# Decode attention with a gated unit: gate's last product in one column tile, the queries' matrix in one load, the output matrix in six

## The chip, the cores and the metric

One core of one Trainium2 chip. Times are microseconds (us) of device time; the profiled execution counts from the start of its span. PE is TensorE, DVE VectorE, ACT ScalarE, POOL GpSimd, SP SyncE, whose queue issues almost all DMA.

## The reference

```python
xn = _layernorm(x)                                   # x: 512
q = (xn @ wq)                                        # 512 -> 32 heads of 128
scores = einsum("bhqd,bhkd->bhqk", q, k_cache) * 128 ** -0.5     # 8192 keys a head
s = softmax(scores) @ v_cache, heads side by side, @ wo          # 4096 -> 512
g = silu((sigmoid(xn @ w_gate) * (xn @ w_up)) @ w_down)          # 512 -> 1376 -> 512
return x + s * g
```

All is float32. One token is decoded, so nearly all time goes into reading the keys, the values and the weights once.

## The kernel before

Three slots in SBUF hold 8 MB each. Heads go in 16 pairs; a pair's keys and a pair's values fill one slot each. Keys alternate between slots 0 and 1, values use slot 2. Before the first keys, slot 2 holds `wq` and then `w_down`, slot 0 holds `w_gate` and `w_up`; at the end `wo` goes into the slot of the pair before the last.

SP issues the loads in program order, each behind a wait that its slot is free: `wq` (two loads, L194 and L197, each with two of the four rows that a partition holds), `w_gate`, `w_up`, keys 0, `w_down` (L322, once all queries are spread), keys 1 (L345, once the product with `w_up` is done), values 0 (L372, once `gated`, the last product of gate, is done), then keys i behind `summed[i - 2]` and values i - 1 behind `valued`. A load waits behind every load ahead of it in this queue.

VectorE first normalizes x (L261 to L280; x itself comes through ACT's queue, L241). It then scales the four rows of `wq` in each partition by x and adds them up in place (`in_place`, L295 to L298, the fourth in eight column pieces at L308), PE sums over partitions and spreads, ACT copies to `q_all`. The same way go `w_gate` and `w_up` (L336 to L344). Then VectorE turns the hidden row into `hid` (L357, L362) and goes on to the scores of pair 0 (L416, L417).

Gate's last product (L365) is 13 matmuls of a 128 x 1 column of `hid` against 128 x 512 of `w_down`, each in one of four column tiles of PE, so that four run side by side and leave four partial rows. ACT copies them (L370), `column_sums` adds them on PE and spreads a quarter of the row on each of four partition groups of `big[1]`, ACT takes the sigmoid (L374), and VectorE multiplies after pair 1 (L462).

At the end `wo` comes as 32 rows of 128 x 512; row r is multiplied by column r of `o_all`. `W_ENDS` says where its loads end. Rows below `W_FOLD` go either to VectorE (`W_DVE`, two chains that are added at L526) or as 1 x 512 products to PE (`W_PE`, with the column tile). `to_fold` (L497) adds both into `s_tmp`; `fold` sums its partitions on PE into `acc`. Rows from `W_FOLD` on go straight into `acc`, a row in four products of 128 columns; the fold stands after the row before the last. VectorE then multiplies by gate and adds x (L548, L550).

PE's notes are recorded by `Later` and played at the end, so all its rows stand at L38.

Of the kernel before, what the change touches and what calls it, by code (L numbers as in the profile page):

```python
# [9 lines left out]
AF = mybir.ActivationFunctionType  # L10
# [3 lines left out]
P = 128  # L14
# [37 lines left out]
def kernel(  # L52
# [14 lines left out]
    D = x.shape[-1]  # L67
    F = w_gate.shape[1]
    KT = D // P
# [3 lines left out]
    NG = 4  # L73
    GP = P // NG
    GC = D // NG
    QT = 512
# [5 lines left out]
    SLOT = NB * Dh  # L82
    HALF = (slice(0, HP), slice(HP, P))

    FP = F // P
    FL = F - FP * P
    FW = FP * GP
    FC = FL // GP
    assert F <= 3 * QT and FL % GP == 0 and 2 * KT * F <= SLOT and (FP + FC) * D <= SLOT // 2

    W_ENDS, W_FOLD = (12, 20, 24, 28, 30, 31, 32), 28
    W_PE = [*zip(range(5), [0] * 5), *zip(range(12, 15), [1] * 3), *zip(range(20, 22), [2] * 2), *zip(range(24, W_FOLD), (0, 1, 2, 3))]
    W_DVE = [r for r in range(W_FOLD) if r not in [r for r, _ in W_PE]]
    V_CUT, K_CUTS = NB // 2, {NP - 2: (NB * 3 // 4,), NP - 1: (NB * 23 // 32,)}

    N_SEMS = 36
    DVE, ACT, SP, POOL = nc.vector, nc.scalar, nc.sync, nc.gpsimd
    PE = Later(nc.tensor)
    pe_only = OrderedEngineSet([nc.tensor.engine])
# [2 lines left out]

    sems = [nc.alloc_semaphore(f"s_{i}") for i in range(N_SEMS)]
    s_out = nc.alloc_semaphore("s_out")

    def sb(name, *shape):
        return nc.alloc_sbuf_tensor(name, [P, *shape], F32)[:]
# [11 lines left out]
    x_row, g_row = sb("x_row", GC), sb("g_row", GC)  # L119
    ones, ident = sb("ones", P), sb("ident", P)  # L120
# [12 lines left out]
    hid = o1[:, :(FP + FC) * GP].rearrange("p (c i) -> p c i", i=GP)  # L133
# [6 lines left out]
    big, po, wide = banks[:2], banks[2], banks[3:]  # L140
# [6 lines left out]
    def semaphore(name):  # L147
        return unused.pop(0)
# [11 lines left out]
    pe, dve, act, pool = (Steps(n) for n in ("s_pe", "s_dve", "s_act", "s_pool"))  # L160
    loads = {}

    def load(eng, name, dst, src, *after):
        wait(eng, *after)
        if name not in loads:
            loads[name] = [semaphore(f"s_{name}"), 0]
        loads[name][1] += 16
        ins = eng.dma_start(dst, src)  # L168
        if not tc.compiled:
            tc.no_tile_sem_insts.add(ins.ins.name)  # L170
        ins.then_inc(loads[name][0], 16)
        return loads[name][0], loads[name][1]

    def wait(eng, *steps):
        for s in steps:
            if s is not None:
                eng.wait_ge(*s)
# [9 lines left out]

    xv = x.rearrange("a b d -> (a b d)")
    wq_t = slots[2].rearrange("p (k c) -> p k c", k=KT)
    wq_v = wq.rearrange("(p k) c -> p k c", k=KT)  # L190
    def load_queries(n):
        return load(SP, f"wq{n}", wq_t[:, n:n + 2, :], wq_v[:, n:n + 2, :])

    ld_wq = [load_queries(0)]  # L194
    tc.close()
    tc.compile()
    ld_wq.append(load_queries(2))  # L197
    wg_t, wu_t = (slots[0][:, n * KT * F:(n + 1) * KT * F].rearrange("p (k f) -> p k f", f=F) for n in range(2))
    ld_g = load(SP, "wg", wg_t, w_gate.rearrange("(p k) f -> p k f", k=KT))
    ld_u = load(SP, "wu", wu_t, w_up.rearrange("(p k) f -> p k f", k=KT))  # L200
# [1 line left out]
    def rows_of(src, i):  # L202
        rows = src.rearrange("b h s d -> (b h s) d")[2 * i * S:2 * (i + 1) * S, :]
        return rows.rearrange("(p j) d -> p (j d)", p=P)
# [8 lines left out]
    def cols(j):  # L213
        return slice(j.start * Dh, j.stop * Dh)
# [7 lines left out]
    def load_values(i, cut, *after):  # L222

        wait(SP, *after)
        for j in cut:
            sem = s_val[j.start // V_CUT]
            SP.dma_start(slots[2][:, cols(j)], rows_of(v_cache, i)[:, cols(j)]).then_inc(sem, 16)  # L227
# [34 lines left out]
    t = dve(DVE.reduce_sum(st[:, 0:1], x_col, axis=AX.X))  # L262
    wait(PE, t)
    t = pe(PE.matmul(pt[:, 0:1], ones, st[:, 0:1], start=True, stop=True))
    wait(DVE, t)
    t = dve(DVE.tensor_scalar(st[:, 1:2], pt[:, 0:1], 1.0 / D, None, op0=ALU.mult))
    wait(DVE, t)
    t = dve(DVE.tensor_scalar(xc, x_col, st[:, 1:2], None, op0=ALU.subtract))
    wait(DVE, t)
    t = dve(DVE.tensor_mul(sq, xc, xc))  # L270
    wait(DVE, t)
    t = dve(DVE.reduce_sum(st[:, 2:3], sq, axis=AX.X))
    wait(PE, t)
    t = pe(PE.matmul(pm[:, 0:1], ones, st[:, 2:3], start=True, stop=True))
    wait(ACT, t)
    t = act(ACT.activation(st[:, 3:4], pm[:, 0:1], AF.Sqrt, bias=eps_t, scale=1.0 / D))
    wait(DVE, t)
    t = dve(DVE.reciprocal(st[:, 4:5], st[:, 3:4]))
# [8 lines left out]
    def in_place(w, k, cols=slice(None)):  # L287
        y = w[:, 0, cols]
        if k == 0:
            return dve(DVE.tensor_scalar(y, y, xn[:, 0:1], None, op0=ALU.mult))  # L290
        return dve(DVE.scalar_tensor_tensor(y, w[:, k, cols], xn[:, k:k + 1], y, op0=ALU.mult, op1=ALU.add))  # L291
# [1 line left out]

    wait(DVE, c_xn)
    for k in range(KT - 1):  # L295
        wait(DVE, ld_wq[k // 2] if k % 2 == 0 else None, t if k else None)
        t = in_place(wq_t, k)
    wait(DVE, t)  # L298
    before_q = PE.take()
# [3 lines left out]
              start=True, stop=True).then_inc(q_spread, 1)  # L303
    each_q = PE.take()
    for t in range(NQ):
        c = slice(t * QT, (t + 1) * QT)
# [4 lines left out]
        for e, h in enumerate(HALF):  # L311
            ins = ACT.copy(qb[h, 2 * t:2 * t + 2, :], q[h, :, e, :])
# [4 lines left out]
    u = slots[2]  # L317
    wd_t = u[:, :FP * D].rearrange("p (c e) -> p c e", e=D)
    wd_rest = u[:, FP * D:(FP + FC) * D]
    wd_last = wd_rest.rearrange("p (c e) -> p c e", e=D)  # L320
    sg, hg, s_gate = (u[:, SLOT // 2 + 3 * n * QT:][:, :w] for n, w in enumerate((F, F, D)))
    load(SP, "wd", wd_t, w_down[:FP * P, :].rearrange("(p r) e -> p r e", r=FP), spread_all)  # L322
    wait(POOL, spread_all)
    c_rest = pool(POOL.memset(wd_rest, 0.0))
    ld_d = load(SP, "wd", wd_last[0:P:NG], w_down[F - FL:, :].rearrange("(p r) e -> p r e", r=FC), c_rest)


    def column_sums(dst, src):
        for g in range(NG):
            ins = PE.matmul(dst[g * GP:(g + 1) * GP, :GC], ones[:, :GP], src[:, g * GC:(g + 1) * GC], start=True, stop=True)  # L330
        return pe(ins)

    rows = []
    chunks = [slice(c, min(c + QT, F)) for c in range(0, F, QT)]
# [1 line left out]
    for dst, src, ld in zip(sums, (wg_t, wu_t), (ld_g, ld_u)):  # L336
        wait(DVE, ld)
        for k in range(KT):
            t = in_place(src, k)
            wait(DVE, t)  # L340
        wait(PE, t, None if rows else (q_free, NK))
        for d, c in zip(dst, chunks):
            ins = PE.matmul(d[:, :c.stop - c.start], ones, src[:, 0, c], start=True, stop=True)
# [3 lines left out]
    for d, c in zip(sums[0], chunks):  # L347
        t = act(ACT.activation(sg[:, c], d[:, :c.stop - c.start], AF.Sigmoid))
    wait(DVE, t, rows[1])
    for d, c in zip(sums[1], chunks):  # L350
        t = dve(DVE.tensor_mul(hg[:, c], sg[:, c], d[:, :c.stop - c.start]))
# [6 lines left out]
    n = FL // NG  # L358
    for g in range(NG):
        r = slice(g * GP, (g + 1) * GP)  # L360
        h = hg[r, NG * FW + g * n:NG * FW + (g + 1) * n].rearrange("p (i c) -> p c i", c=FC)
        t = dve(DVE.transpose(hid[r, FP:, :].rearrange("p c (i m) -> p c i m", m=NG),  # L362
                              h.unsqueeze(3).to_broadcast([GP, FC, n // FC, NG])))
    wait(PE, t, ld_d)
    for c in range(FP + FC):  # L365
        g = c % NG * GP
        ins = PE.matmul(big[0][g:g + 1, :], hid[:, c, 0:1], wd_t[:, c, :] if c < FP else wd_last[:, c - FP, :],
                        start=(c < NG), stop=(c + NG >= FP + FC))
    wait(ACT, pe(ins))
    wait(PE, act(ACT.copy(s_gate, big[0])))  # L370
    gated = column_sums(big[1], s_gate)
    load_values(0, FULL, gated)  # L372
    wait(ACT, gated)
    c_sig = act(ACT.activation(g_row, big[1][:, :GC], AF.Sigmoid))  # L374


    def pair(v):
# [29 lines left out]
    def all_max(i):  # L407
        DVE.wait_ge(turned, i + 1)
        DVE.reduce_max(mx[:1, 1:3], pt[0:1, :].rearrange("o (e p) -> o e p", e=2), axis=AX.X).then_inc(reduced, 1)  # L409
# [31 lines left out]
    for i in range(NP):  # L441
        if i > 0:
            all_max(i - 1)
        if i >= 2:
            k_cut = pieces(*K_CUTS.get(i, ()))
            load_keys(i, k_cut[:1] if i == NP - 1 else k_cut, summed[i - 2])
            if i < NP - 1:
                load_values(i - 1, FULL, (valued, i - 1))
        if i == NP - 1:
            for v in (i - 1, i):  # L450
                load_values(v, V_HALVES[:1], (halved, v))
                load_values(v, V_HALVES[1:], (valued, v))
                if v < i:
                    load_keys(i, k_cut[1:])
        scores(i)
        if i > 0:
            powers_of(i - 1)
            parts(i - 1)
            heads_out(i - 1)
        if i == 1:  # L460
            wait(DVE, c_sig)
            c_gate = dve(DVE.tensor_mul(g_row, g_row, big[1][:, :GC]))  # L462
    all_max(NP - 1)
    powers_of(NP - 1)
    wait(DVE, parts(NP - 1))
# [49 lines left out]
    for k, r in enumerate(W_DVE):  # L515
        n = k % 2
# [3 lines left out]
        if k < 2:  # L520
            ins = DVE.tensor_scalar(part[n], wo_t[:, r, :], col, None, op0=ALU.mult)
        else:
            ins = DVE.scalar_tensor_tensor(part[n], wo_t[:, r, :], col, part[n], op0=ALU.mult, op1=ALU.add)
# [6 lines left out]
    wait(PE, placed)  # L530
    w_rows, w_tiles = zip(*W_PE)
    for k, (r, g) in enumerate(W_PE):
        landed(PE, r, w_rows)
        ins = PE.matmul(big[0][g * GP:g * GP + 1, :], o_all[:, r:r + 1], wo_t[:, r, :],
                        start=(g not in w_tiles[:k]), stop=(g not in w_tiles[k + 1:]))
    folded = to_fold(pe(ins))
    direct = list(range(W_FOLD, WR))
    for r in direct:
        landed(PE, r, direct)
        for g in range(NG):  # L540
            n = copies(g)
            ins = PE.matmul(acc[g * GP:g * GP + n, :], o_all[:, r:r + 1].to_broadcast([P, n]), wo_t[:, r, g * GC:(g + 1) * GC],
                            start=(r == W_FOLD), stop=(r == WR - 1))
# [4 lines left out]
    t = dve(DVE.tensor_mul(g_row, g_row, acc))  # L548
# [66 lines left out]
```

## Time and profile before

| | |
|---|---|
| median of 3 runs | 684.35 us (683.91 to 684.98) |
| profiled execution | 683.9 us, of it span 682.5 us |
| DVE busy | 613.4 us (90%) |
| PE busy | 220.8 us (32%) |
| ACT busy | 44.6 us (7%) |
| read from HBM | 293.67 MB, 430 GB/s over the span |

A timeline row is: start, duration, engine, line, operation, output and input, and in brackets how long the engine stood idle before it and what released it. Consecutive instructions of one kind are merged into a row (x7). PEclk is the granted TensorE clock as a share of 2.4 GHz.

### The profile page before, as it was taken

Reading aid. Unit: us, or ns where it says so; the run is one execution under the profiler, and the core shown is the slowest. Engines: PE = TensorE matmul, PEld = TensorE weight load, DVE = VectorE, ACT = ScalarE, POOL = GpSimd, SP = SyncE. Lnnn points to the kernel's source line nnn. Section 1 sums busy time; section 2 is a strip of 40 time slices with the busy share of each in tenths; the row PEclk is TensorE's granted clock in tenths of the full one; section 3 lists DMA queues with packets and bytes.
Section 4 is the critical chain, followed back from the end, with each engine's and each line's share of the span. In section 5 each row is a group of like instructions: output and inputs, shape, how many; then the busy total and the mean of one; then the engine's idle time right before and its main releaser. Section 6 shows DMA issues by size and latency. Waiting matters only on the chain. (4 is left out here: it accounts for less than half of the span.)

```text
span 682.5 us, 3396 instructions
## 1 busy us (share of the span) xinstructions
PE 220.8 (32%) x1386; PEld 63.9 (9%) x1386; DVE 613.4 (90%) x151; ACT 44.6 (7%) x142; POOL 2.6 (0%) x11
## 2 busy tenths in 40 slices
PE   0353024060513305060512306050412406053368
PEld 0120001010100101010100101010100101011111
DVE  2979999999999998998979899898989899999926
ACT  2130010000000100000000100000010100000010
POOL 0000000000000000000000000000000000000000
PEclk9985658575665758575665758575665858575869
DMA  9999999999999999999999999999999999999998
GB/s 380 430 442 461 442 430 430 430 430 430 430 430 430 430 430 430 438 446 446 453 430 430 430 430 430 430 430 430 430 430 430 430 447 422 475 422 409 436 428 341
DMA packets 6988, 293.68 MB, mean 430 GB/s; under 512 B 798, under 2 KB 812, under 8 KB 1228
## 3 DMA queue, kind: packets, MB, share of 16 engines
q1 hardware_dynamic: 6968, 293.67, 99.5%
q10 hardware_dynamic: 20, 0.01, 0.0%
HBM read 293.67 MB, written 0.00 MB: 430 GB/s over the span
## 5 line engine op out<-in xcount | busy, mean ns | idle before, releaser
L416 DVE TENSOR_TENSOR slot<-slot,q_all 128x16384 f32<-128x16384 f32 (+4 forms) x18 | 275.8, 15323 | 23.6 <-DMA slot<-in_A_k_cache_dram 23.6
L417 DVE TENSOR_REDUCE sc<-slot 128x128 f32<-128x16384 f32 (+4 forms) x18 | 275.8, 15324 | 0.6
L38 PE MATMUL psum<-slot,zeros 128*8 128x512 f32 x1028 | 148.4, 735 | 251.6 <-PEq L38 251.6
L38 PEld LDWEIGHTS psum<-slot,zeros 128*8 128x8 f32 x1028 | 30.7, 103 | 354.9 <-issue 354.9
L38 PE MATMUL psum<-ident,mx 128*1 128x128 f32 x32 | 9.2, 387 | 117.6 <-PEq L38 117.6
L438 ACT COPY o<-psum 128x512 f32<-128x512 f32 x16 | 9.4, 586 | 396.2 <-PE psum L38 396.2
L38 PE MATMUL psum<-slot,ones 128*128 (+3 forms) x36 | 15.8, 614 | 19.2 <-PEq L38 13.8
L38 PE MATMUL psum<-o,pick 128*2 128x128 f32 x128 | 16.5, 272 | 12.8 <-PEq L38 12.8
L291 DVE SCALAR_TENSOR_TENSOR slot<-slot,xn 128x1376 f32<-128x1376 f32 (+1 forms) x8 | 18.9, 2360 | 0.7 <-DMA slot<-in_A_wq_dram 0.4
L424 DVE STREAM_TRANSPOSE psum<-psum 32x128 f32<-32x128 f32 x16 | 4.9, 309 | 9.9 <-PE psum L38 9.9
L429 ACT ACTIVATE nb<-psum 128x2 f32<-128x2 f32 x16 | 2.8, 172 | 160.9 <-PE psum L38 160.9
L38 PEld LDWEIGHTS psum<-ident,mx 128*1 128x1 f32 x32 | 1.8, 80 | 121.8 <-issue 121.8
L431 ACT ACTIVATE zeros<-sc,nb 64x128 f32<-64x128 f32 x32 | 12.8, 400 | 0.9
L38 PEld LDWEIGHTS psum<-o,pick 128*2 128x2 f32 x128 | 9.9, 84 | 29.6 <-issue 27.2
L409 DVE TENSOR_REDUCE mx<-psum 1x2 f32<-1x128 f32 x16 | 4.5, 279 | 8.5 <-PE psum L38 8.5
L38 PE MATMUL psum<-slot,o_all 128*1 128x512 f32 (+2 forms) x60 | 11.3, 423 | 1.1 <-DMA slot<-in_A_wo_dram 1.1
L38 PE MATMUL psum<-zeros,rs 128*32 128x2 f32 x32 | 3.8, 189 | 23.6 <-PEq L38 23.6
L38 PE MATMUL psum<-mx,ones 1*128 1x2 f32 x32 | 8.8, 343 | 7.4 <-PEq L38 7.4
L38 PE MATMUL psum<-slot,o 128*1 128x512 f32 x26 | 5.9, 976 | 13.2 <-DMA slot<-in_B_w_down_dram 13.2
L38 PEld LDWEIGHTS psum<-mx,ones 1*128 1x128 f32 x32 | 7.9, 305 | 14.7 <-issue 14.7
L38 PEld LDWEIGHTS psum<-slot,ones 128*128 128x128 f32 (+1 forms) x36 | 6.3, 203 | 28.4 <-issue 20.7
L261 DVE STREAM_TRANSPOSE g_row<-x_row 128x128 f32<-128x128 f32 x1 | 0.4, 402 | 9.3 <-DMA x_row<-in_A_x_dram 9.3
(54 smaller groups left out, 69.6 us busy)
## 6 DMA issues: line engine op xcount, KB each, us to landing
slot<-in_A_v_cache_dram SPq DMA_DIRECT2D x4, 4096.0 KB, 19.3
slot<-in_A_wq_dram SPq DMA_DIRECT2D x2, 4096.0 KB, 16.3
slot<-in_A_k_cache_dram SPq DMA_DIRECT2D x1, 6144.0 KB, 37.9
slot<-in_A_k_cache_dram SPq DMA_DIRECT2D x1, 5888.0 KB, 37.4
slot<-in_A_wo_dram SPq DMA_DIRECT2D x1, 3072.0 KB, 26.2
slot<-in_B_w_gate_dram SPq DMA_DIRECT2D x1, 2752.0 KB, 26.7
slot<-in_B_w_up_dram SPq DMA_DIRECT2D x1, 2752.0 KB, 32.7
slot<-in_B_w_down_dram SPq DMA_DIRECT2D x1, 2560.0 KB, 23.6
```

Source lines behind the costliest of these rows:

```text
L38: ins = getattr(self.engine, name)(*args, **kwargs)
L261: wait(DVE, dve(DVE.transpose(x_turned, x_row.rearrange("p (i k) -> p k i", k=KT))))
L291: return dve(DVE.scalar_tensor_tensor(y, w[:, k, cols], xn[:, k:k + 1], y, op0=ALU.mult, op1=ALU.add))
L409: DVE.reduce_max(mx[:1, 1:3], pt[0:1, :].rearrange("o (e p) -> o e p", e=2), axis=AX.X).then_inc(reduced, 1)
L416: wait(DVE, dve(DVE.tensor_mul(k[:, j, :], k[:, j, :], qb[:, i:i + 1, :].to_broadcast([P, n, Dh]))))
L417: summed[i] = dve(DVE.reduce_sum(sc[i % 2][:, j], k[:, j, :], axis=AX.X))
L424: turned_out[i] = dve(DVE.transpose(o, pn.rearrange("e (a r) -> e a r", r=WR)))
L429: wait(ACT, act(ACT.mul(nb, pm[:, :2], -SCALE)))
L431: ACT.activation(weights[h, :, e * HT:(e + 1) * HT], sc[i % 2][h].rearrange("p (g b) -> p g b", b=HT), AF.Exp, bias=nb[h, e:e + 1], scale= ...
L438: ACT.copy(o1, po).then_inc(copied, 1)
```

## The change

Three things change. The load of `wq` becomes one load, and the first in-place step waits for all of it. Gate's last product runs its 13 matmuls in column tile 0 alone, with the column of `hid` repeated over 32 output rows, all added in one group in `big[1]`; the copy and `column_sums` go, and the sigmoid and the multiplication become four instructions of 32 partitions, which move each quarter of the row to its partition group. `wo` comes in six loads that end at rows 12, 22, 27, 30, 31 and 32, and the fold starts at row 27.

```diff
-    W_ENDS, W_FOLD = (12, 20, 24, 28, 30, 31, 32), 28
-    W_PE = [*zip(range(5), [0] * 5), *zip(range(12, 15), [1] * 3), *zip(range(20, 22), [2] * 2), *zip(range(24, W_FOLD), (0, 1, 2, 3))]
+    W_ENDS, W_FOLD = (12, 22, 27, 30, 31, 32), 27
+    W_PE = [*zip(range(5), [0] * 5), *zip(range(12, 16), [1] * 4), *zip(range(22, 26), range(NG))]
...
-    ld_wq = [load_queries(0)]
+    ld_wq = load(SP, "wq", wq_t, wq.rearrange("(p k) c -> p k c", k=KT))
     tc.close()
     tc.compile()
-    ld_wq.append(load_queries(2))
...
-        wait(DVE, ld_wq[k // 2] if k % 2 == 0 else None, t if k else None)
+        wait(DVE, t if k else ld_wq)
...
     for c in range(FP + FC):
-        g = c % NG * GP
-        ins = PE.matmul(big[0][g:g + 1, :], hid[:, c, 0:1], wd_t[:, c, :] if c < FP else wd_last[:, c - FP, :],
-                        start=(c < NG), stop=(c + NG >= FP + FC))
-    wait(ACT, pe(ins))
-    wait(PE, act(ACT.copy(s_gate, big[0])))
-    gated = column_sums(big[1], s_gate)
+        ins = PE.matmul(big[1][:GP, :], hid[:, c, 0:1].to_broadcast([P, GP]),
+                        wd_t[:, c, :] if c < FP else wd_last[:, c - FP, :], start=(c == 0), stop=(c == FP + FC - 1))
+    gated = pe(ins)
     load_values(0, FULL, gated)
+    gates = [(g_row[g * GP:(g + 1) * GP, :], big[1][:GP, g * GC:(g + 1) * GC]) for g in range(NG)]
     wait(ACT, gated)
-    c_sig = act(ACT.activation(g_row, big[1][:, :GC], AF.Sigmoid))
+    for dst, src in gates:
+        c_sig = act(ACT.activation(dst, src, AF.Sigmoid))
...
-            c_gate = dve(DVE.tensor_mul(g_row, g_row, big[1][:, :GC]))
+            for dst, src in gates:
+                c_gate = dve(DVE.tensor_mul(dst, dst, src))
```

On SP, at the start of the program (`slot` is the SBUF slot that a load fills):

```order
-L610 UNCONDITIONAL_BRANCH
-L168 DMA slot<-in_A_wq_dram 128x8192
-L196 UNCONDITIONAL_BRANCH
-L168 DMA slot<-in_A_wq_dram 128x8192
+L600 UNCONDITIONAL_BRANCH
+L168 DMA slot<-in_A_wq_dram 128x16384
+L192 UNCONDITIONAL_BRANCH
 L168 DMA slot<-in_B_w_gate_dram 128x5504
 L168 DMA slot<-in_B_w_up_dram 128x5504
```

One load of twice the size stands ahead of the second branch, where one half stood.

On PE, between the products with `w_gate` and `w_up` and the first pair of heads:

```order
 L38 MATMUL psum<-slot,ones 128x352
-L38 MATMUL psum<-slot,o 1x512 x13
-L38 MATMUL psum<-slot,ones 32x128 x4
-L558 UNCONDITIONAL_BRANCH
-L559 BRANCH_PREFETCH_HINT
+L38 MATMUL psum<-slot,o 32x512 x13
+L548 UNCONDITIONAL_BRANCH
+L549 BRANCH_PREFETCH_HINT
 L38 MATMUL psum<-ident,mx 1x128
 L38 MATMUL psum<-mx,ones 128x2
```

The 13 products stay at their place; the four of `column_sums` are gone.

On SP, at the end of the program:

```order
 L168 DMA slot<-in_A_wo_dram 128x6144
-L168 DMA slot<-in_A_wo_dram 128x4096
-L168 DMA slot<-in_A_wo_dram 128x2048 x2
-L168 DMA slot<-in_A_wo_dram 128x1024
+L168 DMA slot<-in_A_wo_dram 128x5120
+L168 DMA slot<-in_A_wo_dram 128x2560
+L168 DMA slot<-in_A_wo_dram 128x1536
 L168 DMA slot<-in_A_wo_dram 128x512 x2
```

The second load grows from 8 rows to 10, the third from 4 to 5; two loads of 4 and 2 rows become one of 3. On VectorE the 14 instructions of `W_DVE` stay 14: rows 5 to 11, then 16 to 21 and 26, where it was 15 to 19, 22 and 23. PE has 13 products of 1 x 512 instead of 14, and five direct rows instead of four.

## Rows read from the trace of the kernel before

**Rows 1.** The page's head, and its row of DMA queue q1 (packets, MB, share of 16 engines)

```profile
span 682.5 us, 3396 instructions
...
q1 hardware_dynamic: 6968, 293.67, 99.5%
```

**Rows 2.** The chain of waits that ended last: start us, us, what

```profile
643.47 35.34 DMA slot<-in_A_wo_dram
```

**Rows 3.** DMA issues of four short stretches: operation, KB, us from issue to landing

```profile
slot<-in_A_wq_dram SPq DMA_DIRECT2D x1, 4096.0 KB, 12.1
...
slot<-in_A_k_cache_dram SPq DMA_DIRECT2D x1, 32.3
...
slot<-in_A_v_cache_dram SPq DMA_DIRECT2D x1, 31.4
...
slot<-in_A_k_cache_dram SPq DMA_DIRECT2D x1, 29.4
```

**Rows 4.** The timeline of SP: start us, us, what

```profile
0.74 1.54 SPq L168 DMA_DIRECT2D slot<-in_A_wq_dram  x2
...
37.27 1.98 SPq L168 DMA_DIRECT2D slot<-in_B_w_down_dram  x2
48.38 0.33 SPq L168 DMA_DIRECT2D slot<-in_A_k_cache_dram  x1
68.60 0.33 SPq L227 DMA_DIRECT2D slot<-in_A_v_cache_dram  x1
89.95 0.33 SPq L168 DMA_DIRECT2D slot<-in_A_k_cache_dram  x1
```

**Rows 5.** The timeline of 11 to 56 us, VectorE

```profile
11.67 0.40 DVE L261 STREAM_TRANSPOSE g_row<-x_row 128x128 f32<-128x128 f32 x1 [9.30 <-DMA x_row<-in_A_x_dram]
...
15.19 2.35 DVE L290 TENSOR_SCALAR slot<-slot,xn 128x4096 f32<-128x4096 f32 x1
17.58 4.49 DVE L291 SCALAR_TENSOR_TENSOR slot<-slot,xn 128x4096 f32<-128x4096 f32 x1
22.50 4.48 DVE L291 SCALAR_TENSOR_TENSOR slot<-slot,xn 128x4096 f32<-128x4096 f32 x1 [0.43 <-DMA slot<-in_A_wq_dram]
...
55.44 17.23 DVE L416 TENSOR_TENSOR slot<-slot,q_all 128x16384 f32<-128x16384 f32 x1
```

**Rows 6.** The timeline of 61 to 68 us: gate's last product

```profile
61.54 5.89 PE L38 MATMUL psum<-slot,o 128*1 128x512 f32 x26 [13.20 <-DMA slot<-in_B_w_down_dram]
62.35 0.15 PEld L38 LDWEIGHTS psum<-slot,o 128*1 128x1 f32 x4 [0.71 <-issue]
```

**Rows 7.** Busy time by stretch: us, engines' busy time, PEclk, DMA share, GB/s

```profile
62.00:66.00 4.00, 4.00 (x24) 0.71 (x17) 4.00 (x1) 0.00 (x0) 0.00 (x0) 0.50 1.21 524
66.00:70.00 4.00, 1.86 (x14) 0.24 (x9) 4.00 (x1) 0.86 (x2) 0.00 (x0) 0.98 0.60 262
670.00:675.00 5.00, 4.71 (x12) 0.76 (x10) 4.36 (x8) 0.00 (x0) 0.00 (x0) 1.00 0.99 421
```

**Rows 8.** The timeline of the tail, 667 to 681 us, VectorE and TensorE

```profile
667.80 0.88 DVE L521 TENSOR_SCALAR q_all<-slot,o_all 128x512 f32<-128x512 f32 x2 [0.73 <-DMA slot<-in_A_wo_dram]
...
667.92 4.45 PE L38 MATMUL psum<-slot,o_all 128*1 128x512 f32 x10
...
672.64 4.73 DVE L523 SCALAR_TENSOR_TENSOR q_all<-slot,o_all,q_all 128x512 f32<-128x512 f32 x7 [0.64 <-DMA slot<-in_A_wo_dram]
...
678.71 0.69 DVE L497 TENSOR_TENSOR q_all<-q_all,psum 128x512 f32<-128x512 f32 x1 [0.62 <-PE psum L38]
...
678.85 1.02 PE L38 MATMUL psum<-slot,o_all 128*32 128x128 f32 x24 [0.20 <-DMA slot<-in_A_wo_dram]
679.45 0.15 PEld L38 LDWEIGHTS psum<-slot,o_all 128*32 128x32 f32 x8 [0.23 <-DMA slot<-in_A_wo_dram]
...
679.68 0.41 PE L38 MATMUL psum<-q_all,ones 128*1 128x128 f32 x8
...
680.08 0.42 PE L38 MATMUL psum<-slot,o_all 128*32 128x128 f32 x8
```

More of the change, by code (lines that the diff above doesn't have):

```diff
@@ L89 @@
     assert F <= 3 * QT and FL % GP == 0 and 2 * KT * F <= SLOT and (FP + FC) * D <= SLOT // 2
-    W_ENDS, W_FOLD = (12, 20, 24, 28, 30, 31, 32), 28
-    W_PE = [*zip(range(5), [0] * 5), *zip(range(12, 15), [1] * 3), *zip(range(20, 22), [2] * 2), *zip(range(24, W_FOLD), (0, 1, 2, 3))]
+    W_ENDS, W_FOLD = (12, 22, 27, 30, 31, 32), 27
+    W_PE = [*zip(range(5), [0] * 5), *zip(range(12, 16), [1] * 4), *zip(range(22, 26), range(NG))]
     W_DVE = [r for r in range(W_FOLD) if r not in [r for r, _ in W_PE]]
     V_CUT, K_CUTS = NB // 2, {NP - 2: (NB * 3 // 4,), NP - 1: (NB * 23 // 32,)}
-    N_SEMS = 36
+    N_SEMS = 34
     DVE, ACT, SP, POOL = nc.vector, nc.scalar, nc.sync, nc.gpsimd
@@ L189 @@
     wq_t = slots[2].rearrange("p (k c) -> p k c", k=KT)
-    wq_v = wq.rearrange("(p k) c -> p k c", k=KT)
-    def load_queries(n):
-        return load(SP, f"wq{n}", wq_t[:, n:n + 2, :], wq_v[:, n:n + 2, :])
-    ld_wq = [load_queries(0)]
+    ld_wq = load(SP, "wq", wq_t, wq.rearrange("(p k) c -> p k c", k=KT))
     tc.close()
     tc.compile()
-    ld_wq.append(load_queries(2))
     wg_t, wu_t = (slots[0][:, n * KT * F:(n + 1) * KT * F].rearrange("p (k f) -> p k f", f=F) for n in range(2))
@@ L320 @@
     wd_last = wd_rest.rearrange("p (c e) -> p c e", e=D)
-    sg, hg, s_gate = (u[:, SLOT // 2 + 3 * n * QT:][:, :w] for n, w in enumerate((F, F, D)))
+    sg, hg = (u[:, SLOT // 2 + 3 * n * QT:][:, :F] for n in range(2))
     load(SP, "wd", wd_t, w_down[:FP * P, :].rearrange("(p r) e -> p r e", r=FP), spread_all)
@@ L325 @@
     ld_d = load(SP, "wd", wd_last[0:P:NG], w_down[F - FL:, :].rearrange("(p r) e -> p r e", r=FC), c_rest)
[L328 to L331, printed above, removed]
     rows = []
```

## The prediction

> **What bounds the kernel now.** I read the page's head and its queue table first. One queue carries 293.67 MB and keeps the 16 DMA engines busy 99.5% of the 682.5 us span [rows 1], so the time is that of one stream of loads, and a change counts in three ways only: the stream starts later or earlier, it runs dry somewhere, or the tail behind its last byte changes. The chain of waits says the same of the end: its longest piece is 35.34 us of waiting for the output matrix [rows 2]. VectorE is the second busiest engine, but all that it does is ahead of the stream by some margin. So next I took the DMA issues and SP's timeline, issue plus time to landing, to see how large each margin is [rows 3, 4]. Values 0 land at 68.60 + 31.4 = 100.0 and keys 2 at 89.95 + 29.4 = 119.35: 8192 KB every 19.35 us. A load that stands behind nothing takes longer than its bytes: the first, 4096 KB, landed 12.1 us after its issue, where 9.68 is its share of the stream. So 8192 KB on an empty queue would land 12.1 + 9.68 = 21.8 us after the issue. A load delays the stream only if its issue plus 21.8 comes out later than its landing before. Last I read the timeline of the three places of the change [rows 5, 6, 8] and the granted clock there [rows 7].
>
> **One load for the queries' matrix.** Its end does not move: the first half landed at 0.74 + 12.1 = 12.84, the second released VectorE at 22.50 [rows 3 to 5], 9.66 us later, which is just the stream's time for 4096 KB. The second issue cost the stream nothing, so saving it gives nothing. No row shows the single load; the bounds are the 2.4 us that the first load took beyond its bytes, gained or paid again, and I take 0, since the one extra issue in the trace cost 0.
>
> The Trainium skill, DMA: Bandwidth & Descriptors (Anatomy of one DMA), gives each DMA a fixed 2.0 us beside its bytes. By that rule two loads fewer (one here, one at the end) would give 4.0 us, an estimate from the page; the same section puts most of it into the write receipt, and 9.66 against 9.68 us agrees that a load behind another hides it.
>
> What moves is VectorE. Its first two in-place steps ran from 15.19 while the second half came, and it then stood idle 0.43 us until 22.50 [rows 5]. Now both start at 22.50 with everything behind them, so all of VectorE's early work comes 22.50 - 15.19 - 0.43 = 6.88 us later: the queries, PE's products with them, the spreading on ACT, the in-place steps of gate, the hidden row, and scores 0, which start at 55.44 + 6.88 = 62.32. On SP four loads are queued behind that, in order:
> - `w_down`, issued 37.27 + 6.88 = 44.15. It is smaller than the 4096 KB that took 12.1, so it would be there by 56.3; it released PE at 61.54 [rows 4, 6]. Covered by keys 0, which are still coming.
> - Keys 1, issued 48.38 + 6.88 = 55.26, plus 21.8 is 77.1; they landed at 48.38 + 32.3 = 80.7. Covered, 3.6 us left.
> - Values 0 hang on gate's product, below.
> - Keys 2 wait for scores 0: 89.95 + 6.88 = 96.83, plus 21.8 is 118.6, against 119.35. This is the thinnest cover, 0.7 us by a cautious count. If it is gone, each us costs a us. Later pairs have more: VectorE needs two passes of 17.2 us a pair where the stream needs 38.7, so it wins back over 3 us a pair.
>
> Cost in the sum: 0.
>
> **Gate's last product in one tile.** Before, 26 instructions (13 products, two passes each) ran four abreast from 61.54: four weight loads every 0.15 + 0.71 = 0.86 us [rows 6], at granted clock 0.50, that is 1.2 GHz, until about 66 us, then at 2.4 GHz [rows 7]. With copy and column sums, the values' issue came at 68.60 [rows 4], 7.1 us after the start. In one tile the same 26 run one after the other: 0.86 us each at 1.2 GHz; at 2.4 GHz the output matrix shows 10 such instructions in one tile in 4.45 us, 0.445 each, at clock 1.00 [rows 7, 8]. That bounds the product by 26 x 0.445 = 11.6 and 26 x 0.86 = 22.4 us. I take what the clock did before: 4.5 us at the lower level (5.2 instructions), the other 20.8 at the higher, 4.5 + 9.3 = 13.8 us. The start is now set by the hidden row at 62.3, not by `w_down` at 61.5, so the end is 76.1, and nothing follows it, copy and sums being gone. Values 0 issued at 76.2 plus 21.8 give 98.0 against 100.0: covered by keys 1, 2 us left. Cost 0. Four sigmoids instead of one and four multiplications instead of one add at most three of each, short ones, on ACT before it waits for scores 0 anyway and on VectorE behind scores 1, when it has begun to win back its 3 us a pair; nothing.
>
> **Six loads for the output matrix.** The bytes and the last load are the same, so row 31 still lands at 680.08 [rows 8]. What changes is when the sum to be folded is ready. VectorE's second group of 7 instructions began at 672.64, at the landing of row 20's load. Rows 12 to 19 took (672.64 - 667.80) / 8 = 0.605 us each to arrive, so a load that ends at row 22 releases VectorE at 667.80 + 10 x 0.605 = 673.85. It again has 7 left, six of this load and row 26, whose load lands at about 676.9, before VectorE is there. 7 instructions took 4.73: 678.6; the sum of the two chains 0.69: 679.3; `to_fold` 0.69: 680.0; it ended at 678.71 + 0.69 = 679.40 before. PE's own part is ready earlier: direct rows 27 to 29 at 678.85, a row of eight instructions taking 0.23 us of issue (679.45 to 679.68), row 30 behind them, so the fold could begin at 679.8. It has to wait for VectorE, to 680.1 with 0.1 for the handover; row 31's products follow 0.23 later, at 680.33 instead of 680.08: +0.25 us, and everything behind is the same. Bounds: 0, if the handover is at its fastest and VectorE gains a little (below it nothing, row 31 lands no earlier), and +0.6, if the handover takes the 0.28 between 679.40 and 679.68 and the fold its whole 0.41. I take +0.25.
>
> **The sum.** 0 + 0 + 0.25. The profiled execution took 683.9 us, so 684.15 by its own measure; the median of the runs shown is 0.45 above it, so 684.6.
>
> **The rivals.**
> 1. TensorE's clock stays at 1.2 GHz through gate's product, because only one of four column tiles works. Then it takes 22.4 us, values 0 are issued at 84.8, landing at 106.6 instead of 100.0: the stream stands dry for 6.6 us and nothing gives it back, since all later loads queue behind: 691.2 us. It decides from 78.2, the last moment for the issue. For it: no row shows a single tile raising the clock. Against it: in the tail a single tile with one output column runs for 5 us at clock 1.00 without losing it [rows 7].
> 2. x comes later. VectorE waited 9.30 us for it [rows 5], its small loads running among those of 32 KB rows. With rows of 64 KB in one load that wait may double: x at 21.0, normalized 3.52 us later (15.19 - 11.67), at 24.5, so VectorE is another 2.0 us late and keys 2 land 118.6 + 2.0 = 120.6, 1.3 us after their time: 685.9. Against: part of the 9.30 is the issue itself and does not grow; up to 22.50 the delay is free, so the wait has to grow by more than 7.3 us.
>  The Trainium skill, DMA: Bandwidth & Descriptors (Queues, rings and completion order), says that an engine changes between queues only behind a whole packet, of 9 to 17 descriptors as a rule; a larger load could so hold x up for longer. The 9.30 us, less than the 12.1 us of the first half, rather show x let in among its rows.
> 3. The stream gains from fewer loads: up to the 2.4 us that the first load took beyond its bytes: 682.2 us. Against it stands the 9.66 us of the second.
>
> **How the numbers follow.** Forecast 80%, rival 1 6%, rival 2 9%, rival 3 3%, another small stall 2%. A difference under 0.2%, 1.37 us, can't be told from none. The forecast's own range is 683.6 to 685.6, from the tail's 0 to 0.6 and the spread of the runs; rival 2 reaches 685.9 and, with the thin cover of keys 2, a bit more. I give 683.5 to 686.4: that leaves out rival 1, most of rival 3 and some of the spread. Within 0.2%: nearly all of the forecast and two thirds of rival 2, 83%; slower 12% (rival 1, the rest of rival 2, other stalls); faster 5%.
>
> **What would show it.** Right: VectorE's first in-place step at about 22.5 and scores 0 at about 62.3; gate's 26 instructions in 13 to 15 us with the clock rising inside; values 0 issued near 76 and keys 2 near 97, their landings at about 100 and 119 as before; a fold that waits for VectorE and row 31's products at about 680.3. Wrong: a clock of 0.50 to the end of gate's product; a first in-place step behind x rather than behind the matrix; a DMA share well under 1 in any stretch around 80 or 100 us; a first load that lands elsewhere than at 22.

## The result, and the profile after

The changed kernel takes 686.53 us (685.23 to 687.48, 7 runs) against 684.34 us (7 runs): ratio 1.0031, interval 1.0022 to 1.0040. Measured once more, beside the experiments, it was 686.77 against 684.40, 1.0033 (1.0021 to 1.0044). It is 2.2 us slower, where 0.25 us was forecast, less than can be told from none. The profiled execution took 686.08 us.

The page's head and queue row [rows 1]:

```profile
span 684.5 us, 3394 instructions
...
q1 hardware_dynamic: 6680, 293.67, 99.3%
```

The span grew by 2.0 us, the bytes not at all. VectorE's timeline [rows 5]:

```profile
15.12 0.40 DVE L256 STREAM_TRANSPOSE g_row<-x_row 128x128 f32<-128x128 f32 x1 [12.76 <-DMA x_row<-in_A_x_dram]
...
22.82 2.35 DVE L285 TENSOR_SCALAR slot<-slot,xn 128x4096 f32<-128x4096 f32 x1 [4.21 <-DMA slot<-in_A_wq_dram]
...
62.84 17.22 DVE L405 TENSOR_TENSOR slot<-slot,q_all 128x16384 f32<-128x16384 f32 x1
```

The first in-place step waits for the matrix, not for x, and scores 0 begin at 62.84, 7.4 us later than before. SP's timeline (keys 1, values 0, keys 2) [rows 4], and the time from issue to landing of values 0, keys 2 and keys 3 (issued at 133.09) [rows 3]:

```profile
55.78 0.33 SPq L168 DMA_DIRECT2D slot<-in_A_k_cache_dram  x1
75.87 0.33 SPq L222 DMA_DIRECT2D slot<-in_A_v_cache_dram  x1
97.34 0.33 SPq L168 DMA_DIRECT2D slot<-in_A_k_cache_dram  x1
```

```profile
slot<-in_A_v_cache_dram SPq DMA_DIRECT2D x1, 24.5
...
slot<-in_A_k_cache_dram SPq DMA_DIRECT2D x1, 23.5
...
slot<-in_A_k_cache_dram SPq DMA_DIRECT2D x1, 26.6
```

Here the loss is seen. Values 0 land at 75.87 + 24.5 = 100.37, before at 100.0: 0.4 late. Keys 2 land at 97.34 + 23.5 = 120.84, before at 119.35: 1.5 late. Keys 3 land at 159.69, 1.7 late: before, they were issued at 125.70, took 32.3 us and landed at 158.0.

```profile
125.70 0.33 SPq L168 DMA_DIRECT2D slot<-in_A_k_cache_dram  x1
```

The first load of the output matrix is still 1.7 late, at 669.49 instead of 667.80. What is lost at keys 2 is never won back. The rest is in the tail [rows 8]:

```profile
669.49 0.88 DVE L511 TENSOR_SCALAR q_all<-slot,o_all 128x512 f32<-128x512 f32 x2 [0.95 <-DMA slot<-in_A_wo_dram]
...
675.55 4.73 DVE L513 SCALAR_TENSOR_TENSOR q_all<-slot,o_all,q_all 128x512 f32<-128x512 f32 x7 [1.86 <-DMA slot<-in_A_wo_dram]
...
681.10 0.69 DVE L487 TENSOR_TENSOR q_all<-q_all,psum 128x512 f32<-128x512 f32 x1
681.85 0.42 PE L38 MATMUL psum<-q_all,ones 128*32 128x128 f32 x8 [0.30 <-DVE q_all L487]
682.07 0.41 PE L38 MATMUL psum<-slot,o_all 128*1 128x128 f32 x8
682.56 0.29 DVE L538 TENSOR_TENSOR g_row<-g_row,psum 128x128 f32<-128x128 f32 x1 [0.77 <-PE psum L38]
```

The fold waits for VectorE, as forecast, and the products of row 31 follow 0.22 us behind it. From the first load's landing to L538 it is 13.07 us, before 680.58 - 667.80 = 12.78: 0.3 us.

Gate's product went as worked out. The timeline row and the clock by stretch [rows 6, 7]:

```profile
62.86 12.98 PE L38 MATMUL psum<-slot,o 128*32 128x512 f32 x26 [7.11 <-DVE o L352]
```

```profile
64.00:66.00 2.00, 2.00 (x3) 0.35 (x2) 2.00 (x1) 0.00 (x0) 0.00 (x0) 0.50 0.76 328
66.00:68.00 2.00, 2.00 (x6) 0.49 (x5) 2.00 (x1) 0.00 (x0) 0.00 (x0) 0.95 0.45 197
```

The clock rose to 2.4 GHz inside a product that uses one column tile, so 26 instructions took 12.98 us (13.8 forecast).

### The profile page after: what moved, and what is told of

It reads as the page before. It is cut to its first block, busy times and chain, and to the rows that moved or that the text cites. A ratio compares the mean times of both kernels' runs of the same rounds, so it can differ in the third digit from the quotient of the medians.

```text
span 684.5 us, 3394 instructions
## 1 busy us (share of the span) xinstructions
PE 230.5 (34%) x1384; PEld 67.1 (10%) x1384; DVE 614.0 (90%) x154; ACT 44.8 (7%) x144; POOL 2.6 (0%) x11
## 5 line engine op out<-in xcount | busy, mean ns | idle before, releaser
L38 PE MATMUL psum<-slot,zeros 128*8 128x512 f32 x1028 | 153.0, 754 | 213.4 <-PEq L38 213.4
L38 PE MATMUL psum<-slot,ones 128*128 (+2 forms) x28 | 15.5, 710 | 22.4 <-PEq L38 17.6
L38 PE MATMUL psum<-slot,o 128*32 128x512 f32 x26 | 13.0, 661 | 7.1 <-DVE o L352 7.1
L513 DVE SCALAR_TENSOR_TENSOR q_all<-slot,o_all,q_all 128x512 f32<-128x512 f32 x12 | 8.1, 748 | 1.9 <-DMA slot<-in_A_wo_dram 1.9
L38 PEld LDWEIGHTS psum<-slot,ones 128*128 128x128 f32 x28 | 6.2, 230 | 30.8 <-issue 24.6
## 6 DMA issues: line engine op xcount, KB each, us to landing
slot<-in_A_wo_dram SPq DMA_DIRECT2D x1, 2560.0 KB, 30.7
```

The lines of the kernel that those rows point to most:

```text
L38: ins = getattr(self.engine, name)(*args, **kwargs)
```

## The experiments

Five theories of the loss are told apart. A: keys 2 are issued too late, since VectorE is late. D: values 0 are as well, in some runs, and the two add up. The rivals are B, the single tile alone; C, the tail; E, that the six loads lose more than the tail once VectorE is late; and that the single load itself disturbs the stream. Each kernel was timed beside the kernel before. The last two columns are the issue and the time from there to landing, from the profile of one execution, in us; the kernel before has 68.60 + 31.4 for values 0, 89.95 + 29.4 for keys 2, and a median span of 683.0 to 683.1 (682.4 to 683.5).

| kernel | us over before (ratio's interval) | span, median (range) | values 0 | keys 2 |
|---|---|---|---|---|
| b_one_load | +0.81 (1.0003 to 1.0021) | 683.9 (682.8 to 685.0) | 69.48 + 30.7 | 97.16 + 24.1 |
| a_two_loads | +0.13 (0.9995 to 1.0013) | 683.2 (682.9 to 683.5) | 74.36 + 25.8 | 91.95 + 27.5 |
| c_one_tile | -0.11 (0.9992 to 1.0010) | 682.9 (682.5 to 683.4) | 75.44 + 24.6 | 89.94 + 29.5 |
| d_six_loads | +3.49 (1.0042 to 1.0070) | 683.1 (682.8 to 683.4) | 68.42 + 31.7 | 90.32 + 29.1 |
| after_again | +2.37 (1.0021 to 1.0044) | 685.25 (683.8 to 685.7) | 75.62 + 24.5 | 97.38 + 23.7 |
| p_load_tile | +0.54 (1.0005 to 1.0023) | 683.4 (682.7 to 685.1) | 75.58 + 24.7 | 95.98 + 23.7 |
| q_load_six | +5.80 (1.0073 to 1.0099) | 685.2 (684.8 to 686.8) | 71.45 + 29.0 | 99.37 + 21.7 |
| e_cover | +1.05 (1.0006 to 1.0024) | 684.1 (683.0 to 684.9) | 75.70 + 24.4 | in halves |
| r_cover_four | -0.05 (0.9992 to 1.0010) | 683.0 (682.8 to 683.4) | 69.27 + 31.0 | in halves |
| t_cover_tile | +0.81 (1.0000 to 1.0018) | 683.8 (682.5 to 684.2) | 77.30 + 24.0 | in halves |
| u_values_late | +1.94 (1.0018 to 1.0037) | 684.95 (683.3 to 685.8) | 77.64 + 23.1 | 91.80 + 28.3 |
| h_delay9 | +3.53 (1.0042 to 1.0069) | 686.5 (685.6 to 688.2) | 68.62 + 32.0 | 101.22 + 21.9 |
| w_mended | +0.30 (0.9999 to 1.0017) | 683.1 (682.9 to 684.0) | in halves | in halves |
| x_mended_seven | +0.12 (0.9995 to 1.0013) | 682.9 (682.6 to 683.3) | in halves | in halves |
| g_delay7 | +2.79 (1.0030 to 1.0058) | 683.4 (683.1 to 685.1) | 69.17 + 31.0 | 98.34 + 22.9 |

In d_six_loads, q_load_six and g_delay7 the time outside the span is 3.8 to 4.9 us in the median, in all others 1.3 to 1.5. Nothing in these runs explains it, so for these three the spans are compared and not the times.

**Each part alone, or taken back.** The edits are the parts of the change as shown above: b_one_load takes the single load alone, c_one_tile the product alone, d_six_loads the output matrix alone; a_two_loads undoes the first in the changed kernel:

```diff
-    ld_wq = load(SP, "wq", wq_t, wq.rearrange("(p k) c -> p k c", k=KT))
+    ld_wq = [load_queries(0)]
...
+    ld_wq.append(load_queries(2))
```

> The kernel before with the single load of the queries' matrix alone. Theory A (VectorE's 7 us delay makes keys 2 be issued too late, the stream runs dry on an engine, and the load itself ends 0.2 to 0.3 us later): 1.3 to 1.9 us slower than before. Theory B (the single column tile makes values 0 late): 0 to 0.3. Theory C (the tail's fold is the loss): 0 to 0.3.

> The changed kernel with the queries' matrix in two loads again, the rest as changed. Theory A: only the tail's delay is left, 0.2 to 0.5 us slower than before. Theory B: 1.5 us or more slower. Theory C: 2 us slower.

> The kernel before with gate's last product in one column tile alone. Theory A: within 0.2 us of before; values 0 are issued near 75 us and still find a full queue. Theory B: 1.5 us slower. Theory C: 0.

> The kernel before with the six loads of the output matrix and the fold at row 27 alone. Theory A: 0.25 to 0.4 us slower, row 31's products held up by VectorE's sum. Theory B: the same. Theory C: 1.5 to 2.2 us slower.

With two loads 0.1 us is left, which can't be told from none. The product alone costs nothing, so B falls; the output matrix alone leaves the span within 0.1 us, so C falls. The single load costs 0.8 in the median, less than the 1.3 to 1.9 that A expected, with spans that spread over 2.2 us: something happens in some runs and not in others.

**Pairs of parts, and keys 2 covered.** p_load_tile keeps `W_ENDS` and `W_FOLD` of before, q_load_six the product in four tiles. e_cover is the changed kernel with scores 0 worked out in two halves, and with

```diff
...
+            if i == 2:
+                for j, after in zip(pieces(NB // 2), (first[0], summed[0])):
+                    load_keys(i, [j], after)
...
```

where `first[0]` is the sum of scores 0's first half.

> The changed kernel once more, beside the three below on one chip. Theory A (keys 2 issued too late for one or more DMA engines, plus the tail): 1.1 to 2.2 us slower than before, an engine's gap near 100 us visible as a later landing of keys 2. Theory D (keys 2 and the late values 0 add up): 1.8 to 2.5.

> The single load of the queries' matrix and gate's product in one tile, with the output matrix in seven loads as before. Theory A: as the single load alone, 0.6 to 1.1 us slower than before. Theory D: 1.5 us or more, since values 0 are issued near 76 us as well. Theory E (the six loads add more than the fold's 0.3 us once engines have fallen apart): 0.6 to 1.1.

> The single load and the six loads of the output matrix, with gate's product in four tiles as before. Theory A: the single load's 0.8 plus the tail's 0.2 to 0.4, so 1.0 to 1.3 us slower. Theory D: the same. Theory E: 1.8 us or more.

> The changed kernel with scores 0 worked out in two halves, and keys 2 loaded in two halves, each issued when its half of the slot is free: the first half goes out near 80 us instead of 97. VectorE is as late as in the changed kernel. Theory A: the stall at keys 2 goes, 0.3 to 0.7 us slower than before is left (the load's later end and the tail). A theory that the single load itself, or x's wait, slows the stream: still about 2 us slower. Theory D: 0.8 to 1.2.

p_load_tile lost 0.5, a little under the 0.6 to 1.1 of A and E and far from D's 1.5; q_load_six fits E's figure by its span (2.2); and e_cover mends a little over half of the loss, as D has it. The profiles show in what the pairs differ. The product with `w_up`, ahead of the hidden row, in p_load_tile and then in q_load_six:

```profile
51.81 2.58 PE L38 MATMUL psum<-slot,ones 128*128 128x512 f32 x6 [3.82 <-DVE slot L286]
```

```profile
52.82 4.95 PE L38 MATMUL psum<-slot,ones 128*128 128x512 f32 x6 [3.82 <-DVE slot L286]
```

The same six instructions take 2.58 us at granted clock 1.00 (2.4 GHz) and 4.95 at 0.50 (1.2 GHz), and 4.11 in the changed kernel, where the clock changed between the two. VectorE waits for them, which is 2.4 us of the 3.4 between the issues of keys 2, at 95.98 and 99.37. These are single executions; why the clock differs from kernel to kernel isn't shown.

E can be read off the same traces: from the landing of the output matrix's first load to the multiplication by gate the six loads take 13.07 us in q_load_six as in the changed kernel, 0.3 more than before, although both streams were late by then. So what q_load_six lost beyond that was lost earlier.

**Which late load costs what.** r_cover_four and t_cover_tile are the single load with e_cover's edit, the product in four tiles and in one, seven loads. u_values_late is c_one_tile with four more products ahead of gate's

```diff
+    for n in range(4):
+        PE.matmul(wide[0][:GP, :], hid[:, 0, 0:1].to_broadcast([P, GP]), wd_t[:, 0, :], start=True, stop=True)
```

and h_delay9 is the kernel before with idle fills on VectorE ahead of scores 0

```diff
+    for n in range(28):
+        wait(DVE, dve(DVE.memset(idle, 0.0)))
```

> The single load with keys 2 in two halves, each issued behind its half of scores 0; gate's product in four tiles and the output matrix in seven loads, as before. Theory A and theory D: keys 2 are the only late load here, so 0 to 0.4 us slower than before, with little spread. A theory that the load of 64 KB rows itself disturbs the stream: 0.8 or more, as the single load alone.

> The same with gate's product in one tile. Theory D: values 0, issued from 75.6 us on depending on the clock, run the stream dry in some runs: 0.3 to 1.2 us slower than before, with a wide spread (spans from 683 to 685). Theory A: 0 to 0.4 as with four tiles.

> The kernel with gate's product in one tile alone, and four further products of the same size ahead of it whose result is not used. Values 0 are issued 3.4 us later, near 78.9. Theory D: a load needs some 3.5 us from issue to the last engine's first row, the engines finish keys 1 from 79.9 on, so 2 to 3 us slower. Theory A: as long as the issue comes before the queue is empty at 80.7 nothing happens: 0.

> The kernel before with some 9 us of idle fills on VectorE ahead of scores 0; two loads of the queries' matrix, four tiles. Keys 2 are issued near 99 us. Theory A and D: every engine runs dry for 1 to 3 us at keys 2, 1.3 to 3 us slower. A theory that the single load is to blame and not VectorE's delay: 0.

r_cover_four has VectorE nearly as late as b_one_load (keys 1 issued at 54.73 against 55.60), one load of 64 KB rows, and no loss. So the load itself does no harm, and keys 2 are all that it costs with four tiles. t_cover_tile adds the single tile and loses 0.8 us with the spread of spans that D expected; its profile shows values 0 late:

```profile
77.30 0.33 SPq L222 DMA_DIRECT2D slot<-in_A_v_cache_dram  x1
```

```profile
slot<-in_A_v_cache_dram SPq DMA_DIRECT2D x1, 24.0
```

They landed at 101.3 instead of 100.0. u_values_late makes only values 0 late, in a kernel with two loads, and is 1.9 us slower, where D had 2 to 3 and A nothing. Its profile is of the shortest of its ten runs (span 683.3), with values 0 landing 0.7 late. In h_delay9 the fills took more than planned (10.85 us, not 9), keys 2 were issued at 101.22, and the span grew by 3.5.

**Both covered.** w_mended is e_cover with

```diff
+    load_values(0, V_HALVES[1:], t)
     wait(PE, t, ld_d)
...
-    load_values(0, FULL, gated)
+    load_values(0, V_HALVES[:1], gated)
```

x_mended_seven the same with seven loads. g_delay7 is h_delay9 with 17 fills.

> The changed kernel with both thin covers mended: keys 2 in two halves behind the halves of scores 0, and values 0 in two halves, the upper one issued as soon as the hidden row is turned (near 63 us), the lower one behind gate's product. VectorE is as late as in the changed kernel, the six loads stay. Theory D (late issues of keys 2 and values 0 are the whole loss beside the tail): 0.2 to 0.5 us slower than before, spans within 0.8 us of each other. Theory E (the six loads lose more than the tail once VectorE is late): 1 us or more.

> The same with the output matrix in seven loads and the fold at row 28, as before. Theory D: 0 to 0.2 us slower than before, narrow. Theory E: the same; its difference to the kernel with six loads would then be 1 us or more instead of 0.3.

> The kernel before with idle fills of some 6.8 us on VectorE ahead of scores 0, the delay that the single load causes; two loads, four tiles, seven loads. Keys 2 are issued near 96.8. Theory D: as the single load alone, 0.4 to 1.2 us slower than before. If the single load costs something of its own beside the delay: 0 to 0.3.

SP's timeline of w_mended:

```profile
57.47 0.33 SPq L168 DMA_DIRECT2D slot<-in_A_k_cache_dram  x1
64.53 13.54 SPq L222 DMA_DIRECT2D slot<-in_A_v_cache_dram  x2
81.97 17.65 SPq L168 DMA_DIRECT2D slot<-in_A_k_cache_dram  x2
```

Its VectorE was later than the changed kernel's (keys 1 at 57.47 instead of 55.78), and yet only 0.3 us over before is left, 0.1 with seven loads. That rules E out. The 0.2 us between the two, the six loads' share, is no more than the noise; the spans of w_mended spread over 1.1 us, where 0.8 was expected. Part of it may be lost at keys 3: in its profile they were issued at 135.04 and landed 23.2 us later, 0.2 behind before, with one engine idle for 0.3 us ahead of them by the packet records. g_delay7, with nothing changed but VectorE's delay, has a median span 0.4 us longer, just what D expected at the least, and two of its five 2 us longer. No kernel here beats the kernel before by more than can be measured.

## Why the prediction was wrong

What held: the stream as the bound; VectorE's shift (6.88 forecast, 7.4 measured: the matrix released it 0.3 later, the product with `w_up` took 0.3 longer); gate's product and the issue of values 0 (76.2 forecast, 75.87); x, which was later by 3.5 us but not too late; the tail (0.25 forecast, 0.3 in the trace, 0.1 to 0.2 by time). The rule on whole packets of the Trainium skill (DMA: Bandwidth & Descriptors, Queues, rings and completion order) did not decide: x still came in at 15.12, between the rows of a matrix that was there at 22.8. Nor did its 2.0 us for each DMA, which the section (Anatomy of one DMA) gives for DMAs issued from GpSimd, where these are SP's: d_six_loads has one load fewer than before and the same median span, 683.1.

The step that failed is the test of cover: "A load delays the stream only if its issue plus 21.8 comes out later than its landing before." By it values 0 had 2 us left and keys 2 0.7, both at no cost. The 21.8 is right for a queue that has run dry: keys 2 landed 21.7 us after the issue in q_load_six, where all 16 engines had stood idle, this row:

```profile
slot<-in_A_k_cache_dram SPq DMA_DIRECT2D x1, 21.7
```

and 21.9 in h_delay9. Wrong was to infer that a load which comes a little before the queue is empty costs nothing. In the changed kernel 97.34 + 21.8 is 119.1, in time for a landing at 119.35 or, with values 0 0.4 late, 119.7; it landed at 120.84. The queue is served by 16 engines, each with its own rows. No view shows them one by one, but the packet records of the traces can be chained (each row to the one that ended as it began; the records name no engine): in the changed kernel one engine of 16 ends its rows of values 0 at 100.0 and gets its first row of keys 2 at 101.18, 3.8 us after the issue; the other 15 go on with gaps of 0.2 us at most. That one engine is late by 1.2 us, each load has landed only when all 16 have, and no engine pauses again to let it catch up. In t_cover_tile three engines stood idle ahead of values 0, the longest 0.9 us; in g_delay7 five ahead of keys 2, the longest 1.7 us; in r_cover_four none at either place. When every engine had run dry, in h_delay9, the first rows came 1.0 to 1.8 us after the issue. So an issue into a nearly empty queue reached its last engine later than one into an empty queue. Why is open; no run took it apart. The idle time is not all: in b_one_load, q_load_six, g_delay7 and h_delay9 first rows of keys 2 also took 2.6 to 3.6 us instead of 2.42, in the changed kernel 2.5 at most.

The second mistake was to shift all by one number. TensorE's clock at the product with `w_up` moves the issue of keys 2 by over 2 us from kernel to kernel, so a cover of 0.7 us is no cover; and the price came twice, at keys 2 (0.8 us in b_one_load) and at values 0 (0.8 in t_cover_tile), with 0.1 to 0.2 for the tail. The sum, 1.7 to 1.8, is 0.4 to 0.7 short of the 2.2 to 2.4 measured. The stalls differ in size from run to run, so the parts need not simply add, and the remainder can't be assigned. Rival 2 had the place, VectorE's lateness at keys 2, but x as its cause, which was not it.

## What to carry to other kernels

Where one stream of loads bounds a kernel, look at each load's time from issue to landing before a change that moves its issue. Here the kernels in which values 0 and keys 2, of 8192 KB each, both took 24.6 us or longer lost nothing clear; those whose profile has one of them at 24.4 or less lost 0.4 to 3.5 us in the median; and at 21.7 and 21.9 all engines had run dry. A profile is one execution, though: that of e_cover, with 24.4, lost next to nothing itself. By these kernels a cover under some 2.8 us (an estimate, 24.6 - 21.8) is not safe, since one late engine of 16 holds up all that follows. If the producer can't be earlier, load in halves: the half whose slot is free first refills the queue, and the delay cost nothing here (r_cover_four, x_mended_seven).

## What the runs showed that I had not expected

- A load that is issued while the engines still have rows reaches its last engine later (3.2 to 3.8 us after the issue in b_one_load, after_again and the changed kernel, by the packet records) than one that finds them all idle (1.8 us in h_delay9, its first engine at 1.0).
- The granted clock rises while a single column tile works, from 0.50 to 0.95 between 64 and 68 us.
- Doubling the rows of the matrix from 32 to 64 KB held up x's small loads by 3.5 us (9.30 to 12.76): by the packet records their steps on an engine came 1.24 us apart before and 2.42 after, the time of one row of the matrix.
- The time outside the span can differ by 3.5 us (1.4 before, 4.9 in d_six_loads) between kernels that differ in a few instructions; this stays unexplained.
